# Decay bias rows made on GpSimd by one multiply-add instead of on ScalarE and VectorE

## The chip, the cores and the metric

The kernel runs on one core of a Trainium2 chip. The metric is the device time of one launch in microseconds (us); smaller is better. Engine names are those of the profile: PE is TensorE's matmul side and PEld its weight load, DVE is VectorE, ACT is ScalarE, POOL is GpSimd, SP is SyncE, which here only issues DMAs.

## What is computed

Attention with a decay bias (batch 8, 8 heads, 576 tokens, head width 64), followed by a gated feed forward (512 to 1536 to 512) over the 4608 tokens:

```python
scores = matmul(q, k.T) / sqrt(D)
cum    = cumsum(maximum(s, 0), axis=-1)
bias   = -(cum[..., :, None] - cum[..., None, :])       # query i, key j: cum[j] - cum[i]
scores = where(j > i, -1e9, scores + minimum(bias, 0))
attn   = softmax(scores) ; x = attn @ v                 # heads side by side: 4608 x 512
out    = ((sigmoid(x @ w_gate) * (x @ w_val)) @ w_out)
```

`cum` never falls along the tokens, so at every key that a query may see (j <= i) the bias is at most 0 before the minimum is taken, up to rounding.

## The kernel before, in words

There are 64 heads (8 batches of 8). A head is worked in five query tiles of 64, 128, 128, 128 and 128 queries, which see 64, 192, 320, 448 and 576 keys. One tile is one tick of the loop at L643, so there are 320 ticks, and three stages of a tile lie one tick apart: the score products on PE (`s_part`, L358) with the bias row (`bias_part`, L369); the sum of scores and bias with its extreme on DVE (L385) and the exponential on ACT (L390), both in `max_part`; the split of the weights into fp16 high and low parts (L401 to L404) and their transposes by DMA in `p_part`. The value products (`av_part`, L415) come a head later.

The first batch, heads 0 to 7, goes another way in float32, with functions whose names begin with `n_` (`n_bias` L494, `n_max` L502), because the feed-forward weights are prepared in the same stretch of time: per hidden block, loads, squares on ACT (L224), a sum over the partitions on POOL (`partition_all_reduce`, L228), and the split on DVE and ACT (L231 to L245). The sum over the partitions is also used for each pair of later heads, to find the scale of q and k (`qk_square`, L297), and once per batch for v (L143). That is 12, 28 and 8 of them.

From batch 1 on, the feed forward of the batch before is worked beside the attention: 216 units in all (18 groups of 256 tokens by 12 hidden blocks), each of 24 matmuls at L586, a tanh on ACT (L591), a product on DVE (L593), a split on ACT and DVE (L596, L597) and 6 matmuls at L610 three units later. The schedule gives some three units to a head. The last batch's feed forward stands alone at the end. Results leave by DMAs issued on POOL (L615), which also issues the loads of v for its squares (L138).

**The bias row.** For head i and query tile t, a row of `cum` (`crow`, loaded onto all partitions by L338) is combined with one value per partition, the query's own `cum`. Heads 8 to 63 (`bias_part`): ACT computes `relu(cf * crow + bc)` (L374), with `cf` and `bc` from `qk_scale`, in the units of the scaled scores and with the sign turned. Heads 0 to 7 (`n_bias`): DVE computes `min(crow - cumT, 0)` (L497). In both, POOL then fills the part of the last 64 or 128 columns above the diagonal with a large value (`affine_select`, L375 and L498), and DVE reads the row at L385 or L508. The rows have the tag `rl`, two buffers, which the loads of v at L138 share.

**What sets the order.** The Python code gives the emission order and marks some pieces as urgent (`first()`); a scheduler then places each engine's instructions. Every engine works its own list strictly in that order. Around the bias row the lists to watch are POOL's (row, diagonal fill, sums over the partitions, DMA issues), DVE's (L385 stands among the feed forward's L593 and L597) and PE's (score products among feed-forward units). Scores have three PSUM banks, the products `gv` of L586 two.

Of the kernel before, what the change touches and what calls it, by code (L numbers as in the profile page):

```python
# [17 lines left out]
P = 128  # L18
GT = 256          # tokens of one feed-forward group
PSCALE = 2.0 ** 14  # scale of the split softmax weights  # L20
# [4 lines left out]
def tile_attention_then_gated_ffn(  # L25
# [19 lines left out]
    QP = 96                  # tokens per chunk of q and k  # L45
    QC = S // QP
    # query tiles: (first query, queries, keys seen)
    TILES = [(0, 64, 64)] + [(64 + 128 * i, 128, 192 + 128 * i) for i in range(4)]
    NTL = len(TILES)
    QA = 320                 # queries of the first half of the value product  # L50
    QB = S - QA
    JA, JB = 3, 5            # key blocks of the two halves
    HI_ACT = (2, 3, 4)       # query tiles whose high weights ScalarE writes
    NN = H                   # heads computed in float32
    LAG = 3                  # units between the two products of the feed forward
# [15 lines left out]
    w1 = [cp.tile([P, NC, 2, 2, P], F16, name=f"w1_{f}") for f in range(NF)]   # chunk, gate/val, hi/lo  # L71
    w2 = [cp.tile([P, 2, DM], F32R, name=f"w2_{f}") for f in range(NF)]        # hi/lo
# [10 lines left out]
    expo = cp.tile([P, 2], F32, name="expo")     # exponents of -scale(q) and scale(k)  # L83
# [7 lines left out]
    nc.gpsimd.memset(cumT, 0.0)  # L91
    cum_d = dp.tile([NH, S], F32, name="cum_d")
# [4 lines left out]
    def field(ss, n, tag):  # L97
        """Exponent field of the power of two that brings a norm (from its square) to 2**15 at most."""
        e = wp.tile([P, n], I32, tag=f"xe{n}", name=f"xe_{tag}")
        f_ = wp.tile([P, n], I32, tag=f"xf{n}", name=f"xf_{tag}")  # L100
        nc.vector.tensor_scalar(e, ss.bitcast(I32), 23, None, ALU.logical_shift_right)
        nc.vector.tensor_scalar(f_, e, -0.5, 204.75, ALU.mult, ALU.add)
        return f_
# [19 lines left out]
    for t, (q0, m, w) in enumerate(TILES):  # L123
        ps = score_bank(f"pct{t}")
        nc.tensor.transpose(ps[:m, :NH], cum[:, q0 : q0 + m], ident[:NH, :NH])
        nc.vector.tensor_copy(cumT[:m, t, :], ps[:m, :NH])

# [1 line left out]
    vch = H * S * D // P // S      # chunks of a batch of v  # L129
    vview = v.rearrange("b h s d -> b (h s d)").rearrange("b (c p n) -> b c p n", c=vch, p=P)  # L130
    sv = {}        # batch -> (scale, inverse)
# [33 lines left out]
    scb = {}       # batch -> [P, 2, NF] factors of the gate and value products  # L165
# [3 lines left out]
    # staging: two buffers of their own, and the last weights' room until they come  # L169
# [34 lines left out]
    def decode_weight(n):  # L204
        """float32 from the words of a float64: exponents below the normal range end at zero."""
# [94 lines left out]
    def qk_scale(p):  # L300
# [8 lines left out]
        cf = wp.tile([P, 3], F32, tag="qkcf", name=f"qkcf{p}")       # -1/c, 1/c, c  # L309
# [59 lines left out]
    def bias_part(i, t):  # L369
        q0, m, w = TILES[t]  # L370
        p, j = divmod(i, 2)
        sc, cf, bc = qkc[p]
        r = wp.tile([P, S], F32, tag="rl", name=f"rl{i}_{t}")
        nc.scalar.activation(r[:m, :w], crow[i][:m, :w], AF.Relu, bias=bc[:m, t, j : j + 1], scale=cf[:m, 0:1])  # L374
        nc.gpsimd.affine_select(r[:m, q0:w], r[:m, q0:w], pattern=[[-1, m]], compare_op=ALU.is_ge,  # L375
                                fill=MASKED, base=0, channel_multiplier=1)
        rl[i, t] = r
# [81 lines left out]
    def n_prep(p):  # L459
        """Transposes of q (a tile per head, the other head's rows zero) and k of a pair of heads."""  # L460
# [33 lines left out]
    def n_bias(i, t):  # L494
        q0, m, w = TILES[t]
        r = wp.tile([P, S], F32, tag="rl", name=f"rl{i}_{t}")
        nc.vector.tensor_scalar(r[:m, :w], crow[i][:m, :w], cumT[:m, t, i : i + 1], 0.0, ALU.subtract, ALU.min)  # L497
        nc.gpsimd.affine_select(r[:m, q0:w], r[:m, q0:w], pattern=[[-1, m]], compare_op=ALU.is_ge,  # L498
                                fill=-MASKED, base=0, channel_multiplier=1)
        nB[i, t] = r  # L500
# [138 lines left out]
    NE, NOFF = 44, 80        # ticks: the feed forward begins, and has caught up  # L639
    FPT = 1.5                # units of the feed forward in a tick when it begins  # L640
    WLA = 3                  # hidden blocks whose weights are made ahead
    nticks = NTL * NH
    for n in range(nticks + 6):  # L643
# [17 lines left out]
        # value products of the head before  # L661
# [5 lines left out]
        # preparation of the heads to come  # L667
# [48 lines left out]
        # feed forward of the batch before  # L716
# [16 lines left out]
        b = m // (NTL * H) if m >= 0 else 0    # batches whose heads have all been written  # L733
# [39 lines left out]
```

## Time and profile before

| what | us |
|---|---|
| three runs | 1253.43, 1255.73, 1258.74; median 1255.73 |
| span of the profiled execution, first to last instruction | 1250.6 |
| busy in it: PE, PEld | 1168.5, 928.8 |
| busy in it: ACT, DVE | 979.2, 910.2 |
| busy in it: POOL | 180.0 |

The profiled execution has no timed run of its own; its span is 5.1 us under the median of the runs. "Busy" is the time in which an engine's instructions ran; a matmul's end is modelled. Groups are named by line, engine, operation and tiles (out<-in). In a timeline row the first number is the start in us from the beginning of the span, the second the time that the row's instructions took, and the bracket the engine's idle time ahead of it with what ended it ("issue": nothing that the profile shows). In a row of windows each engine's busy us come with the count of its instructions, then the granted clock of TensorE as a share, the share of the DMA engines that is busy, and GB/s.

### The profile page before, as it was taken

How to read it: one execution, taken by the hardware profiler on the slowest of the kernel's cores; microseconds unless marked ns; L12 is line 12 of the kernel's file. 1: busy time of each engine (PE TensorE's matmuls, PEld its weight loads, DVE VectorE, ACT ScalarE, POOL GpSimd, SP SyncE). 2: the span in 40 equal slices, each digit the busy share in tenths (PEclk: the TensorE clock that was granted, in tenths of full speed). 3: DMA queues.
4: the chain of work that ended last, by engine and by line, in shares of the span. 5: the costliest groups of instructions: out<-in, count | busy, mean ns of one | idle time of the engine just before them, and what ended most of it. 6: DMA issues, size and time to landing. Idle time of an engine off the chain costs nothing. (4 is left out here: it accounts for less than half of the span.)

```text
span 1250.6 us, 26501 instructions
## 1 busy us (share of the span) xinstructions
PE 1168.5 (93%) x8581; PEld 928.8 (74%) x8581; DVE 910.2 (73%) x3167; ACT 979.2 (78%) x2453; POOL 180.0 (14%) x463
## 2 busy tenths in 40 slices
PE   2688979999999999999999999999999999999997
PEld 1566757776777777788888877777778788888885
DVE  5898889788889787877676677878888788522221
ACT  4888879899989898988777688889998998533221
POOL 2333111111111121110111011111121111000000
PEclk9788789999999999999999999999999999999999
DMA  8765788778897898865475488768887865200000
GB/s 230 216 182 156 171 159 167 156 135 160 165 172 137 141 169 152 163 135 123 118 128 120 84 156 150 155 133 163 155 165 140 150 136 120 44 18 17 2 18 17
DMA packets 434731, 164.98 MB, mean 132 GB/s; under 512 B 400928, under 2 KB 420384, under 8 KB 434592
## 3 DMA queue, kind: packets, MB, share of 16 engines
q1 hardware_dynamic: 414752, 125.53, 54.2%
q0 software_dynamic: 5440, 18.88, 5.1%
q10 hardware_dynamic: 14400, 18.88, 5.1%
q8 instruction: 67, 1.10, 0.4%
q14 instruction: 72, 0.59, 0.2%
HBM read 75.64 MB, written 9.58 MB: 68 GB/s over the span
## 5 line engine op out<-in xcount | busy, mean ns | idle before, releaser
L586 PE MATMUL gv<-xg,w 128*128 128x256 f16 x5184 | 618.9, 274 | 3.1 <-ACT xg L562 1.6
L586 PEld LDWEIGHTS <-w 128*128 128x128 f16 x5184 | 496.8, 98 | 85.9 <-issue 20.9
L610 PE MATMUL o<-w,h 128*128 128x512 f32 x1296 | 360.0, 411 | 2.6 <-ACT osb L614 2.6
L610 PEld LDWEIGHTS o<-w,h 128*128 128x128 f32 x1296 | 227.2, 189 | 43.0 <-ACT osb L614 3.5
L591 ACT ACTIVATE th<-gv,scb 128x256 f32<-128x256 f32 (+3 forms) x288 | 111.2, 412 | 98.2 <-PE gv L586 96.8
L375 POOL TENSOR_SCALAR_AFFINE_SELECT rl<-rl 64x64 f32<-64x64 f32 x280 | 91.7, 328 | 668.9 <-ACT rl L374 524.6
L404 DVE SCALAR_TENSOR_TENSOR p<-e,er,p 64x128 f16<-64x128 f32 (+1 forms) x280 | 169.9, 613 | 17.2 <-ACT p L401 14.6
L374 ACT ACTIVATE rl<-cr,qkb,qkcf 64x64 f32<-64x64 f32 x280 | 180.0, 643 | 0.6 <-DVE em L385 0.4
L390 ACT ACTIVATE e<-e,em 64x64 f32<-64x64 f32 x280 | 154.8, 553 | 17.6 <-DVE em L385 16.8
L593 DVE SCALAR_TENSOR_TENSOR t<-th,gv 128x256 f32<-128x256 f32 x216 | 89.2, 413 | 102.3 <-ACT th L591 101.5
L596 ACT ACTIVATE h<-t,scb 128x256 fp32r<-128x256 f32 (+3 forms) x288 | 121.5, 447 | 41.6 <-DVE t L593 41.4
L597 DVE SCALAR_TENSOR_TENSOR h<-t,scb,h 128x256 fp32r<-128x256 f32 (+3 forms) x288 | 114.8, 412 | 50.1 <-ACT h L596 48.1
L385 DVE CUSTOM_DVE_ANT_0 e<-s,rl,qkcf 64x64 f32<-64x64 f32 x280 | 132.8, 482 | 20.9 <-PE s L366 12.9
L401 ACT ACTIVATE p<-e,er 128x384 f16<-128x384 f32 x168 | 118.8, 711 | 1.3 <-ACT e L390 0.9
L424 PEld LDWEIGHTS <-v 128*128 128x128 f16 (+1 forms) x896 | 79.4, 97 | 44.3 <-issue 16.5
L365 PE MATMUL s<-T 128*64 128x64 f16 x336 | 92.9, 289 | 7.4 <-DVE em L385 5.0
L366 PE MATMUL s<-T 128*64 128x64 f16 x336 | 92.5, 281 | 6.3 <-DMA T<-T 6.3
L294 ACT ACTIVATE jq<-qk 96x768 f16<-96x768 f32 x56 | 46.9, 837 | 35.2 <-DMA qk<-in_q_dram 33.9
L424 PE MATMUL av<-ptb,v 128*128 128x256 f16 (+2 forms) x560 | 64.2, 252 | 10.4 <-DVE x L431 5.7
L365 PEld LDWEIGHTS <-T 128*64 128x64 f16 x336 | 33.2, 99 | 53.1 <-issue 44.4
L396 DVE TENSOR_SCALAR er<-es 64x1 f32<-64x1 f32 x280 | 40.9, 147 | 32.3 <-ACT e L390 29.0
L431 DVE SCALAR_TENSOR_TENSOR x<-av,xh 64x320 f32<-64x320 f32 x112 | 50.7, 453 | 16.6 <-ACT xh L430 14.8
(152 smaller groups left out, 1253.3 us busy)
## 6 DMA issues: line engine op xcount, KB each, us to landing
cr<-cum_d SPq DMA_DIRECT2D x64, 288.0 KB, 3.8
vsq<-in_v_dram POOLq DMA_DIRECT2D x32, 288.0 KB, 3.8
out_dram<-osb POOLq DMA_DIRECT2D x36, 256.0 KB, 3.4
v<-in_v_dram SPq DMA_DIRECT2D x64, 128.0 KB, 2.7
qk<-in_q_dram SPq DMA_DIRECT2D x28, 288.0 KB, 3.9
qk<-in_k_dram SPq DMA_DIRECT2D x28, 288.0 KB, 4.8
T<-T SPq DMA_DIRECT2D x112, 72.0 KB, 2.1
ws<-in_moe_w_out_dram ACTq DMA_DIRECT2D x8, 512.0 KB, 4.5
```

What stands on the lines that cost most here:

```text
L365: nc.tensor.matmul(ps[:m, : b_ - a], lhs, T[i][:, 1, a:b_], start=True, stop=False)
L374: nc.scalar.activation(r[:m, :w], crow[i][:m, :w], AF.Relu, bias=bc[:m, t, j : j + 1], scale=cf[:m, 0:1])
L385: nc.vector.tensor_tensor_reduce(e_t[t][:m, a:b_], ps[:m, : b_ - a], rl[i, t][:m, a:b_], c, init, ALU.add, ALU.min, acc[:m])
L390: nc.scalar.activation(e_t[t][:m, :w], e_t[t][:m, :w], AF.Exp, bias=init, scale=-1.0, accum_out=sm[:m])
L401: nc.scalar.activation(hi, e, AF.Copy, scale=d[:m, 1:2])
L404: nc.vector.scalar_tensor_tensor(p_t[t][:m, :, 1], e, d[:m, 1:2], hi, ALU.mult, ALU.subtract)
L424: nc.tensor.matmul(ps[:, lo:n], lhs, PT[i][half][:kk, kb, hl, lo:n], start=(kb == 0 and hl == 0), stop=(kb == nj - 1 and hl == 1))
L586: nc.tensor.matmul(ps[:, gv, :n], w1[f][:, cc, gv, wl], xg[g][:, cc, xl, :n], start=(c == 0), stop=(c == 3 * NC - 1))
L591: nc.scalar.activation(th[:, a:e], ps[:, 0, a:e], AF.Tanh, scale=scb[b][:, 0, f : f + 1])
L596: nc.scalar.activation(h[:, 0, a:e], t2[:, a:e], AF.Copy, scale=scb[b][:, 1, f : f + 1])
L597: nc.vector.scalar_tensor_tensor(h[:, 1, a:e], t2[:, a:e], scb[b][:, 1, f : f + 1], h[:, 0, a:e].bitcast(F32), ALU.mult, ALU.subtract)
L610: nc.tensor.matmul(ps[:m], h[:, hl, tt * P : tt * P + m], w2[f][:, wl], start=(f == 0 and c == 0), stop=(f == NF - 1 and c == 2))
```

## The change

Both ways to make the bias row become one `tensor_scalar` on POOL with two per-partition values. In `bias_part` it is `crow * cf + bc`, without the relu; in `n_bias` it is `crow * 1 + cumN`, without the minimum, where `cumN` is `-cumT` of the first eight heads, made once on DVE. The diagonal fill stays behind it on POOL. Nothing else in the code differs but comments.

```diff
     cumT = cp.tile([P, NTL, NH], F32, name="cumT")
     nc.gpsimd.memset(cumT, 0.0)
+    cumN = cp.tile([P, NTL, NN], F32, name="cumN")
...
         nc.vector.tensor_copy(cumT[:m, t, :], ps[:m, :NH])
+    nc.vector.tensor_scalar(cumN, cumT[:, :, :NN], -1.0, None, ALU.mult)
...
         r = wp.tile([P, S], F32, tag="rl", name=f"rl{i}_{t}")
-        nc.scalar.activation(r[:m, :w], crow[i][:m, :w], AF.Relu, bias=bc[:m, t, j : j + 1], scale=cf[:m, 0:1])
+        nc.gpsimd.tensor_scalar(r[:m, :w], crow[i][:m, :w], cf[:m, 0:1], bc[:m, t, j : j + 1], ALU.mult, ALU.add)
         nc.gpsimd.affine_select(r[:m, q0:w], r[:m, q0:w], pattern=[[-1, m]], compare_op=ALU.is_ge,
                                 fill=MASKED, base=0, channel_multiplier=1)
...
         r = wp.tile([P, S], F32, tag="rl", name=f"rl{i}_{t}")
-        nc.vector.tensor_scalar(r[:m, :w], crow[i][:m, :w], cumT[:m, t, i : i + 1], 0.0, ALU.subtract, ALU.min)
+        nc.gpsimd.tensor_scalar(r[:m, :w], crow[i][:m, :w], 1.0, cumN[:m, t, i : i + 1], ALU.mult, ALU.add)
         nc.gpsimd.affine_select(r[:m, q0:w], r[:m, q0:w], pattern=[[-1, m]], compare_op=ALU.is_ge,
                                 fill=-MASKED, base=0, channel_multiplier=1)
```

The code's lines behind `cumN` stand two or three numbers later in the changed kernel: L228 becomes L230, L297 becomes L299, L375 becomes L378, L385 becomes L388.

POOL's list near the beginning, before: the first sum over the partitions (`wtot`) and the first bias rows of head 0 (`rl`). A row that says only "ISA" is an instruction without tiles.

```order
L228 ISA
L228 ISA wtot0_572<-wss0_476 128x2
L498 AFFINE_SELECT rl0_0_203<-rl0_0_203 64x64
L498 AFFINE_SELECT rl0_1_212<-rl0_1_212 128x128
L138 DMA vsq0_0_230<-in_v_dram 128x576
L498 AFFINE_SELECT rl0_2_235<-rl0_2_235 128x128
L138 DMA vsq0_1_246<-in_v_dram 128x576
L228 ISA wtot1_874<-wss1_779 128x2
```

The same place in the changed kernel:

```order
L230 ISA
L230 ISA wtot0_574<-wss0_478 128x2
L500 ISA
L500 TENSOR_SCALAR rl0_0_205<-cr0_170,cumN_125 64x64
L500 TENSOR_SCALAR rl0_1_214<-cr0_170,cumN_125 128x192
L501 AFFINE_SELECT rl0_0_205<-rl0_0_205 64x64
L501 AFFINE_SELECT rl0_1_214<-rl0_1_214 128x128
L140 DMA vsq0_0_232<-in_v_dram 128x576
L500 TENSOR_SCALAR rl0_2_237<-cr0_170,cumN_125 128x320
L501 AFFINE_SELECT rl0_2_237<-rl0_2_237 128x128
L230 ISA
L230 ISA wtot1_876<-wss1_781 128x2
```

Besides the multiply-adds, the change puts a bare ISA row ahead of the first multiply-add behind a sum over the partitions, and another ahead of each sum that follows a multiply-add. Before, there is one such row ahead of the first sum, one ahead of the very first `affine_select` (`ident`, a helper's line) and one at the program's start; `affine_select` and the sums then stand side by side without any.

POOL's list in the middle, before: the end of head 27 and the start of head 28, with the sum for heads 30 and 31 (`qkt15`).

```order
L375 AFFINE_SELECT rl27_3_6882<-rl27_3_6882 128x128
L297 ISA qkt15_7269<-ssq1_119 128x2
L375 AFFINE_SELECT rl27_4_6960<-rl27_4_6960 128x128
L375 AFFINE_SELECT rl28_0_7033<-rl28_0_7033 64x64
L375 AFFINE_SELECT rl28_1_7061<-rl28_1_7061 128x128
```

The same place in the changed kernel:

```order
L378 AFFINE_SELECT rl27_3_6884<-rl27_3_6884 128x128
L140 DMA vsq4_1_6912<-in_v_dram 128x576
L377 TENSOR_SCALAR rl27_4_6962<-cr27_6495,qkcf13_6229,qkb13_6233 128x576
L299 ISA
L299 ISA qkt15_7271<-ssq1_119 128x2
L378 AFFINE_SELECT rl27_4_6962<-rl27_4_6962 128x128
L377 ISA
L377 TENSOR_SCALAR rl28_0_7035<-cr28_6780,qkcf14_6790,qkb14_6794 64x64
L378 AFFINE_SELECT rl28_0_7035<-rl28_0_7035 64x64
L377 TENSOR_SCALAR rl28_1_7063<-cr28_6780,qkcf14_6790,qkb14_6794 128x192
```

Here a bare row stands ahead of the sum and another behind the diagonal fill of `rl27_4`, so two consecutive bias rows (`rl27_4`, `rl28_0`) each have one in front. In the whole list there are 47 bare rows at the lines of the sums (11, 28 and 8 of them at L230, L299 and L145) and 47 at those of the multiply-adds (11 at L500 and 36 at L377).

DVE's list at the same place in the changed kernel, from the product of a feed-forward unit on (`t2`, `h` are the feed forward's, `e_4` with `rl27_4` is the sum of scores and bias):

```order
L596 SCALAR_TENSOR_TENSOR t2_4_7_6943<-th4_7_6940,gv4_7_6915 128x256
L388 ISA e_4_94,em27_4_0_7040<-s27_4_0_6956,rl27_4_6962,qkcf13_6229 128x288
L388 ISA em27_4_0_7040 128x1
L407 SCALAR_TENSOR_TENSOR p16_3_98<-e_3_93,er27_3_7046,p16_3_98 128x4x128
L388 ISA e_4_94,em27_4_1_7042<-s27_4_288_6959,rl27_4_6962,em27_4_0_7040,qkcf13_6229 128x288
L388 ISA em27_4_1_7042 128x1
L600 SCALAR_TENSOR_TENSOR h4_7_6945<-t2_4_7_6943,scb1_3570,h4_7_6945 128x128
```

It is nearly the list of before: the sum that reads the bias row stands ahead of the feed forward's next split (`h4_7`). On PE, from head 19 on, the count of feed-forward matmuls ahead of a tile's score product is that of before or at most 24 matmuls, one unit, off.

## The prediction

> **What bounds the kernel now.** I read the page's first part, then the windows of three stages: the first batch with the weights (A), the attention of batches 1 to 7 beside the feed forward (B), and the last feed forward alone (C).
>
> ```profile
> span 1250.6 us, 26501 instructions
> PE 1168.5 (93%) x8581; PEld 928.8 (74%) x8581; DVE 910.2 (73%) x3167; ACT 979.2 (78%) x2453; POOL 180.0 (14%) x463
> 30.00:140.00 110.00, 88.32 (x465) 68.06 (x466) 98.43 (x332) 93.71 (x256) 33.44 (x62) 0.83 0.64 175
> 140.00:1085.00 945.00, 916.26 (x6936) 728.00 (x6937) 758.50 (x2709) 826.94 (x2062) 136.86 (x367) 0.99 0.75 145
> 1085.00:1251.00 166.00, 157.47 (x1160) 128.98 (x1158) 37.64 (x93) 46.73 (x112) 4.35 (x8) 0.98 0.04 14
> ```
>
> In A, DVE is busy for 98.43 of 110 us, and TensorE's granted clock is 0.83. In B, PE is busy for 916.26 of 945 us at clock 0.99, while ACT (88%) and DVE (80%) keep up. So B, three quarters of the span, is set by PE, and an engine matters there only where PE comes to wait for it. POOL works for 14% of the time; but it works its list in order, and every bias row goes through it.
>
> **What leaves ACT and DVE.** The groups, of DVE and of ACT:
>
> ```profile
> L497 DVE TENSOR_SCALAR rl<-cr,cumT 64x64 f32<-64x64 f32 (+4 forms) x40 | 14.7, 377 | 4.4 <-ACT vsq L139 4.4
> L374 ACT ACTIVATE rl<-cr,qkb,qkcf 64x64 f32<-64x64 f32 x280 | 180.0, 643 | 0.6 <-DVE em L385 0.4
> ```
>
> DVE loses 40 instructions, 14.7 us, all in A; one small product for `cumN` comes back, under half a us by the 377 ns of this row. ACT loses 280 instructions, 180.0 us, all in B. What that could bring at most: in A the 14.7 us, since DVE is the bound there; in B not the 180 but PE's idle 945 - 916.26 = 28.7 us. Together 43, and I would expect some 27 of them (the 14.7, and under half of PE's gaps, as many of those wait for transfers or other products).
>
> **What POOL gets: the multiply-adds.** The trace has none on POOL. Its nearest rows there are the diagonal fill, which also reads and writes a float32 row, and the fills of constants:
>
> ```profile
> L375 POOL TENSOR_SCALAR_AFFINE_SELECT rl<-rl 128x128 f32<-128x128 f32 x224 | 76.0, 340 | 568.3 <-ACT rl L374 458.0 <-DVE er L397 32.1 <-DVE p L404 17.1
> L375 POOL TENSOR_SCALAR_AFFINE_SELECT rl<-rl 64x64 f32<-64x64 f32 x56 | 15.7, 280 | 100.6 <-ACT rl L374 66.7 <-DVE er L397 31.9 <-DVE er L396 1.4
> L468 POOL MEMSET nq<- 64x576 f32 x8 | 4.8, 611 | 1.4 <-PE s L491 1.2
> L91 POOL MEMSET cumT<- 128x320 f32 x1 | 0.4, 354 | 0.0
> ```
>
> From 64 to 128 columns the fill grows by 60 ns, 0.94 ns a column on a start of 220; the constants grow by (611 - 354) / 256 = 1.0 ns. At 0.94 the five multiply-adds of a head (64 to 576 columns, 1600 in all) take 5 x 220 + 1600 x 0.94 = 2.6 us. That is an estimate, its lower end the start alone (1.1 us), its upper end twice it (5.2). Even the upper end with the fills of a head ((76.0 + 15.7) / 56 = 1.6 us) is 6.8 us of the 945 / 56 = 16.9 us that a head takes in B. By themselves the multiply-adds fit, and cost nothing on the path: POOL makes a row while PE works for the tile before.
>
> **What POOL gets beside them: the bare rows.** This carries the forecast. A sum over the partitions and a multiply-add never follow each other without a bare ISA row between. Before, there is one ahead of `ident` and one ahead of the first sum. POOL's timeline shows what follows them:
>
> ```profile
> 1.77 0.10 POOL L85 MEMSET expo<- 128x1 f32 x1
> 13.71 0.28 POOL masks.py:199 TENSOR_SCALAR_AFFINE_SELECT ident<-ident 128x128 f32<-128x128 f32 x1 [11.84 <-issue]
> 14.44 2.51 POOL L468 MEMSET nq<- 64x576 f32 x4
> 23.62 0.50 POOL L228 PARTITION_ALL_REDUCE wtot<-wss  x1 [6.67 <-ACT nk L481]
> ```
>
> Between the end of the constants and `ident`, whose row in the order stands right behind the first bare row, POOL stands still for 11.84 us, with nothing that the profile would show as waited for. Behind the second, it stands still for 6.67 us, to 16.95 + 6.67 = 23.62. There the squares that the sum needs came late as well:
>
> ```profile
> 23.09 0.19 ACT L224 ACTIVATION_READ_ACCUMULATOR w<-w 128x1 f32 x1
> ```
>
> They end at 23.28, so 6.67 us is an upper bound for that row and no price. I read a bare row as a change of POOL's set of operations. The Trainium skill states it so (GPSIMD Engine Reference, section Instruction dispatch): operation libraries are loaded at run time, and the first call to a freshly loaded one pays some 6 us (5.95 measured) with no instruction of its own in the profile. The gap of 11.84 us marked "issue" agrees in kind and is twice as long; no row here separates a load in the middle of the kernel.
>
> The transfers were busier behind the first bare row than in B, which I take as the reason to expect less than 11.84 later:
>
> ```profile
> 2.00:12.00 10.00, 0.00 (x0) 0.00 (x0) 2.34 (x3) 2.61 (x3) 0.00 (x0) 1.00 1.07 314
> 17.00:23.30 6.30, 2.87 (x10) 1.69 (x10) 4.92 (x10) 5.04 (x13) 0.00 (x0) 1.00 0.78 221
> ```
>
> The DMA share was 1.07 there, 0.78 behind the second and is 0.75 in B. Prices: the row ahead of a sum, between 0 and 6.67 us, taken as 6; the row ahead of a multiply-add, between 0 and 11.84, taken as 8, between the two gaps and nearer to the one at B's DMA share. A pair is 14 us, bounds 0 to 18.5. By the Trainium skill's 5.95 (the section just named) for each it would be 11.9 us.
>
> **How much of a pair is covered.** A bias row is ready shortly before DVE takes it. For two rows of head 27 (POOL's fill, then DVE's sum):
>
> ```profile
> 448.90 0.29 POOL L375 TENSOR_SCALAR_AFFINE_SELECT rl<-rl 128x128 f32<-128x128 f32 x1 [0.55 <-ACT rl L374]
> 450.63 0.42 DVE L385 CUSTOM_DVE_ANT_0 e<-s,rl,qkcf 128x192 f32<-128x192 f32 x1
> 454.35 0.30 POOL L375 TENSOR_SCALAR_AFFINE_SELECT rl<-rl 128x128 f32<-128x128 f32 x1 [5.16 <-ACT rl L374]
> 454.94 0.55 DVE L385 CUSTOM_DVE_ANT_0 e<-s,rl,qkcf 128x320 f32<-128x320 f32 x1
> ```
>
> The lead is 1.4 and 0.3 us. That this was no hindrance shows in the waits of DVE (us in total, times, longest):
>
> ```profile
> DVE e L385 <- POOL rl L375: 5.3, 8, 2.9
> ```
>
> Two `rl` buffers allow at most two tiles, 2 x 945 / 280 = 6.8 us. When DVE waits at L385, the feed forward's L593 and L597 stand behind it on DVE, so PE runs out of free `gv` banks after about one more unit, whose 24 matmuls take 2.8 us:
>
> ```profile
> 450.32 2.78 PE L586 MATMUL gv<-xg,w 128*128 128x256 f16 x24
> ```
>
> So between 0.3 and 6.8 + 2.8 = 9.6 us of a pair is hidden; I take 5. Where a pair lies in front of two consecutive bias rows, as for `rl27_4` and `rl28_0`, its parts add up, as DVE has one tile to work in between. After it PE cannot make up anything: it was the bound.
>
> **The sum.** B has 36 pairs (the bare rows at L377), each worth 14 - 5 = 9 us: 324. A has 11 (L500): 99. A's gain on DVE and ACT's relief count nothing here, since both then wait. PE's clock: at A's share of idle time it was 0.83, in B 0.99. With 324 us of waits B falls toward A's state; 0.94 would cost 916.26 x (0.99 / 0.94 - 1) = 49, nothing and 916.26 x (0.99 / 0.83 - 1) = 177 being the ends; I take 50. The span is 1250.6 + 324 + 99 + 50 = 1723.6, and with the 5.1 us between the span and the median of the runs 1729, forecast as 1730. By the Trainium skill's 11.9 us a pair (the same section) the same sum is 1250.6 + 47 x 6.9 + 50 + 5.1 = 1630.
>
> **The rivals.**
>
> *The bare rows are cheap, and the change wins.* For it: the 11.84 us stand at the start, where the transfers are at their busiest and where much happens once; the 6.67 us hide behind ACT. Then the row costs less than the cover, POOL has room, A loses 14.7 us of DVE, and B some of PE's gaps: 1255.73 - 27 = 1229. It decides where a pair takes less than about 5 us in the middle of the kernel. Against it: nothing else stands in that gap of 11.84 us. Chance 0.06.
>
> *The bare rows are cheap, but POOL and DVE get in each other's way.* Diagonal fills took longer in A than in B:
>
> ```profile
> L498 POOL TENSOR_SCALAR_AFFINE_SELECT rl<-rl 128x128 f32<-128x128 f32 x32 | 18.1, 576 | 34.3 <-DVE rl L497 26.0 <-DVE xg__326 L110 2.6 <-DVE xf_w L102 1.7
> L404 DVE SCALAR_TENSOR_TENSOR p<-e,er,p 64x128 f16<-64x128 f32 (+1 forms) x280 | 169.9, 613 | 17.2 <-ACT p L401 14.6
> ```
>
> The same fill took 576 ns instead of 340, beside a DVE that hardly rested. If each of the 320 multiply-adds holds an instruction of DVE like L404 up for such a 0.24 us, or is held up by it, that is 76 us: 67 of them in B, where DVE would be at 758.5 + 67 = 826 of 945 and PE still the bound, and 9 in A, which take most of the 14.7 back. The result is 1250, no difference to be measured. The Trainium skill has the rule (SBUF — State Buffer, section Who interferes with whom): a DVE instruction with two SBUF inputs and a GpSimd instruction that reads SBUF take turns over a shared port, the later one waiting fully. It bears on this rival alone. Chance 0.05, of which 0.02 with a visible loss.
>
> *POOL becomes the bound.* If both kinds of bare row cost what the trace shows at the start, a pair takes 18.5 us: 47 x 13.5 = 635, and with the clock at 0.90 another 916.26 x (0.99 / 0.90 - 1) = 92, so 1250.6 + 635 + 92 + 5.1 = 1983. In A alone the 11 pairs would be 204 us of POOL, in a stage of 110. Chance 0.17.
>
> **How the numbers follow.** The forecast has 0.72. Its own range goes from 9.5 us a pair (47 x 4.5 = 212 and 25 for the clock: 1490) to 16.5 (47 x 11.5 = 541 and 90: 1890). The range that should hold the time 8 times in 10 goes on to the third rival's value, 1990, and below to 1440, a pair of 9 us with no loss of clock; the two cheap rivals and the outer parts of the others are left out, some 0.2. About 0.5% is what a measurement of this kernel can tell from no change. Faster by more: 0.06, the first rival. Within it: 0.03, of the second. Slower: 0.72 + 0.17 + 0.02 = 0.91.
>
> **What would show it.** On POOL, idle time of several us ahead of each first multiply-add behind a sum, and ahead of each sum, marked "issue" or put down to an instruction long done; the multiply-adds themselves at 0.3 to 0.8 us. On DVE, a long wait of L388 for POOL's `rl`, against 5.3 us before. In B, PE busy for some 73% instead of 97%, gaps of 5 to 12 us near the end of every second head, and a granted clock under 0.99. ACT's busy time falls by 180 us with no gain. The forecast is wrong if POOL goes on within 2 or 3 us of a bare row, if the gaps lie elsewhere than behind them, or if multiply-adds take several us each.

## The result, and the profile after

The changed kernel takes 1620.74 us (median, 1615.26 to 1621.96) where the kernel before takes 1254.58 (1249.35 to 1258.74). The ratio is 1.2898, 95% interval 1.2853 to 1.2943: it is slower by 29%, some 366 us. The profiled execution spans 1619.3 us, 368.7 more than that of before.

The page of the changed kernel, its first part, and then the windows of the three stages, with edges at the same events as before (first batch, batches 1 to 7, last feed forward). The columns are those of the windows above: PE, PEld, DVE, ACT, POOL, granted clock, DMA share, GB/s.

```profile
span 1619.3 us, 26532 instructions
PE 1252.9 (77%) x8581; PEld 978.4 (60%) x8581; DVE 917.2 (57%) x3128; ACT 853.0 (53%) x2173; POOL 445.6 (28%) x783
```

```profile
30.00:255.00 225.00, 114.00 (x472) 88.00 (x471) 95.64 (x304) 100.10 (x267) 56.46 (x101) 0.59 0.31 90
255.00:1453.00 1198.00, 973.00 (x6924) 756.44 (x6923) 766.95 (x2694) 693.32 (x1770) 378.04 (x645) 0.91 0.59 113
1453.00:1619.00 166.00, 158.19 (x1166) 129.47 (x1163) 37.95 (x93) 46.83 (x113) 4.35 (x8) 0.99 0.04 14
```

No engine is busy for more than 77% of the time. Stage A has grown by 115 us (225 against 110), B by 253 (1198 against 945), C not at all. In B, PE is idle for 1198 - 973 = 225 us against 28.7 before, 196 more, and its same work takes 973 - 916 = 57 us longer, at clock 0.91 instead of 0.99. That is where the 368 us are.

What PE and DVE stand for is in the list of waits of the changed kernel, of which these are some lines (us in total, times, longest):

```profile
POOL rl L377 <- issue: 183.8, 26, 7.5
POOL qkt L299 <- issue: 148.0, 24, 7.2
DVE qk L304 <- POOL qkt L299: 122.2, 28, 6.6
PE s L367 <- DVE em L388: 97.3, 33, 9.0
DVE vso L147 <- POOL vst L145: 84.5, 8, 13.0
POOL wtot L230 <- issue: 64.4, 10, 7.6
POOL rl L500 <- issue: 64.2, 9, 8.1
DVE xe_w L102 <- POOL wtot L230: 56.6, 11, 6.7
DVE e L388 <- POOL rl L378: 51.2, 22, 7.2
DVE e L388 <- POOL rl L377: 20.0, 4, 7.0
```

In the kernel before, the first of the waits for a sum was short:

```profile
DVE qk L302 <- POOL qkt L297: 18.6, 19, 2.2
```

POOL stands still some 6 to 8 us at a time for "issue", at the lines of the multiply-adds (L377, L500) and of the sums (L299, L230, L145). In the trace's records, from the bare row to the next instruction, it is 5.8 us (median) ahead of a sum and 7.1 ahead of a multiply-add, 47 of each: 12.9 us a pair. DVE stands mostly for the sums: L304, L147 and L102 add up to 263 us, against 25 before, while its wait for the bias row itself (L388) is 51.2 and 20.0, 71 us. PE then waits for DVE's `em`.

No row shows what POOL does in these gaps: the two DMA queues of instructions move 67 and 72 packets in the kernel before and in the changed one alike, though the changed one has 92 more such gaps. "Load" below is the prediction's reading of them; what the trace shows is the bare row and the time until the next instruction.

One pair in the middle, on POOL's timeline (start, us, what it was, idle before it and what ended that):

```profile
1207.72 0.82 POOL L377 TENSOR_SCALAR rl<-cr,qkcf,qkb 128x576 f32<-128x576 f32 x1
1214.99 0.41 POOL L299 PARTITION_ALL_REDUCE qkt<-ssq  x1 [6.45 <-issue]
1215.29 0.36 POOL L378 TENSOR_SCALAR_AFFINE_SELECT rl<-rl 128x128 f32<-128x128 f32 x1
1223.23 0.56 POOL L377 TENSOR_SCALAR rl<-cr,qkcf,qkb 64x64 f32<-64x64 f32 x1 [7.59 <-ACT qk L327]
```

The first gap, 6.45 us, stands at the change to the sums' set, the second, 7.59 us, at the change back. The second is put down to an instruction of ACT, L327, which scales q and k and writes nothing that this multiply-add reads: so a load can hide in a list of waits behind another engine's name. DVE in the same time:

```profile
1209.36 0.14 DVE L400 RECIPROCAL er<-er 128x1 f32<-128x1 f32 x1
1215.43 0.24 DVE L304 TENSOR_SCALAR qk<-qkt 128x2 int32<-128x2 int32 x1 [5.92 <-POOL qkt L299]
...
1225.49 0.42 DVE L388 CUSTOM_DVE_ANT_0 e<-s,rl,qkcf 128x192 f32<-128x192 f32 x1 [0.58 <-POOL rl L378]
```

And PE:

```profile
1211.11 1.14 PE L427 MATMUL av<-ptb,v 128*128 128x256 f16 x10
1212.19 2.80 PE L589 MATMUL gv<-xg,w 128*128 128x256 f16 x24
1214.74 1.64 PE L613 MATMUL o<-w,h 128*128 128x512 f32 x6
...
1217.62 0.24 PE L367 MATMUL s<-T 128*128 128x192 f16 x1 [1.06 <-DVE em L388]
...
1224.96 0.35 PE L367 MATMUL s<-T 128*128 128x448 f16 x1 [2.71 <-DVE em L388]
```

While DVE stands for the sum, PE still has value products, one feed-forward unit and the second products of another, and it runs dry at the end of that and again at the end of the second load: here 1.06 + 2.71 = 3.8 us of the two gaps reach it.

The groups of POOL's two operations at the later heads (count, then busy us, mean ns, idle before; a group is named by its smallest shape):

```profile
L377 POOL TENSOR_SCALAR rl<-cr,qkcf,qkb 64x64 f32<-64x64 f32 x280 | 228.0, 817 | 535.0 <-DVE em L388 258.3
L378 POOL TENSOR_SCALAR_AFFINE_SELECT rl<-rl 64x64 f32<-64x64 f32 x280 | 107.7, 393 | 10.8
```

A multiply-add takes 817 ns in the mean, 4.1 us a head, and the fill behind it 393 ns where it took 328.

### The profile page after: what moved, and what is told of

Same layout as the page of the kernel before. It is cut to its first block, busy times and chain, and to the rows that moved or that the text cites. A ratio compares the mean times of both kernels' runs of the same rounds, so it can differ in the third digit from the quotient of the medians.

```text
span 1619.3 us, 26532 instructions
## 1 busy us (share of the span) xinstructions
PE 1252.9 (77%) x8581; PEld 978.4 (60%) x8581; DVE 917.2 (57%) x3128; ACT 853.0 (53%) x2173; POOL 445.6 (28%) x783
## 5 line engine op out<-in xcount | busy, mean ns | idle before, releaser
L589 PE MATMUL gv<-xg,w 128*128 128x256 f16 x5184 | 646.3, 282 | 25.3 <-DVE t L596 12.8
L589 PEld LDWEIGHTS <-w 128*128 128x128 f16 x5184 | 510.1, 101 | 119.4 <-issue 31.2
L613 PE MATMUL o<-w,h 128*128 128x512 f32 x1296 | 367.3, 419 | 54.5 <-ACT osb L617 54.5
L377 POOL TENSOR_SCALAR rl<-cr,qkcf,qkb 64x64 f32<-64x64 f32 x280 | 228.0, 817 | 535.0 <-DVE em L388 258.3
L613 PEld LDWEIGHTS o<-w,h 128*128 128x128 f32 x1296 | 233.9, 194 | 108.2 <-ACT osb L617 66.0
L388 DVE CUSTOM_DVE_ANT_0 e<-s,rl,qkcf 64x64 f32<-64x64 f32 x280 | 132.0, 481 | 86.9 <-POOL rl L378 51.2
L367 PE MATMUL s<-T 128*64 128x64 f16 x336 | 97.3, 301 | 100.5 <-DVE em L388 97.3
L427 PEld LDWEIGHTS <-v 128*128 128x128 f16 (+1 forms) x896 | 86.4, 104 | 85.4 <-issue 55.5
L494 PE MATMUL s<-nk,nq 128*128 128x288 f32 (+4 forms) x96 | 50.5, 641 | 84.6 <-DVE em L511 82.3
L378 POOL TENSOR_SCALAR_AFFINE_SELECT rl<-rl 64x64 f32<-64x64 f32 x280 | 107.7, 393 | 10.8
L427 PE MATMUL av<-ptb,v 128*128 128x256 f16 (+2 forms) x560 | 70.5, 267 | 44.5 <-DVE x L434 29.8
L368 PE MATMUL s<-T 128*64 128x64 f16 x336 | 96.5, 295 | 2.7 <-DMA T<-T 2.7
L494 PEld LDWEIGHTS s<-nk,nq 128*128 128x128 f32 (+1 forms) x96 | 22.0, 279 | 97.4 <-DVE em L511 90.2
```

The costliest lines, as they stand in the source:

```text
L368: nc.tensor.matmul(ps[:m, : b_ - a], lhs, T[i][:, 2, a:b_], start=False, stop=True)
L377: nc.gpsimd.tensor_scalar(r[:m, :w], crow[i][:m, :w], cf[:m, 0:1], bc[:m, t, j : j + 1], ALU.mult, ALU.add)
L388: nc.vector.tensor_tensor_reduce(e_t[t][:m, a:b_], ps[:m, : b_ - a], rl[i, t][:m, a:b_], c, init, ALU.add, ALU.min, acc[:m])
L427: nc.tensor.matmul(ps[:, lo:n], lhs, PT[i][half][:kk, kb, hl, lo:n], start=(kb == 0 and hl == 0), stop=(kb == nj - 1 and hl == 1))
L589: nc.tensor.matmul(ps[:, gv, :n], w1[f][:, cc, gv, wl], xg[g][:, cc, xl, :n], start=(c == 0), stop=(c == 3 * NC - 1))
L613: nc.tensor.matmul(ps[:m], h[:, hl, tt * P : tt * P + m], w2[f][:, wl], start=(f == 0 and c == 0), stop=(f == NF - 1 and c == 2))
```

## The experiments

Theory 1 is the prediction's: the price is the loading of POOL's sets of operations, wherever a sum and a multiply-add follow each other. Theory 2, the rival: the price is the multiply-adds themselves, because POOL and DVE hold each other up (the second rival of the prediction, at several times its price), or because POOL makes the rows later than ACT did. All ratios are against the kernel before on the same chip.

**The sums moved to PE, so that nothing is switched.** Two kernels: the changed one, and the one before as its control, each with every sum over the partitions made by two matmuls with ones and a copy on DVE. For q and k this sum also moves, from `qk_square` to `qk_scale`.

```diff
+    def total(tot, src, n, name):
+        ps = pp.tile([P, 512], F32, tag="gv", name=f"sum_{name}")
+        for h_ in range(2):
+            nc.tensor.matmul(ps[64 * h_ : 64 * h_ + 64, :n], ones, src, start=True, stop=True)
+        nc.vector.tensor_copy(tot, ps[:, :n])
...
-        nc.gpsimd.partition_all_reduce(tot, vss[b], P, ADD_REDUCE)
+        total(tot, vss[b], vch, f"v{b}")
```

> The changed kernel with all 48 sums over the partitions taken off POOL: each is a float32 product with a matrix of ones on TensorE and a copy on DVE, so that POOL keeps the multiply-adds and has no bare row between kinds of operations. Theory 1 (the time went into the changes of POOL's set of operations, 5.8 and 7.1 us each by the trace): nothing is left to wait for, the loss of 366 us goes altogether, and the kernel stands at 1225 to 1255 us, a little under before if the relief of ScalarE and VectorE is worth anything. Theory 2 (the multiply-adds themselves are too slow on POOL, 0.82 us a piece, or hold VectorE's two-input instructions up at the memory port): the loss stays for the most part, 1450 us or more. In between, 1300, would say that both take a share.

> Control: the kernel before with the same sums on TensorE and nothing else changed, so bias rows as before on ScalarE and VectorE. Both theories: within 1% of before, 1243 to 1262 us. What e1 differs from this one by is the multiply-adds' own effect, without any change of operation sets.

Measured: 1388.07 us for the changed kernel (ratio 1.1059, 1.1002 to 1.1116) and 1363.2 for the control (1.0874, 1.0827 to 1.0922). The control misses its range by 100 us, so the edit does something of its own, and the first number can't be read by itself. What it does is in the control's windows:

```profile
270.00:300.00 30.00, 30.00 (x229) 24.72 (x227) 6.83 (x15) 7.35 (x15) 0.99 (x2) 1.00 0.05 19
300.00:400.00 100.00, 59.26 (x322) 35.70 (x321) 67.57 (x265) 74.31 (x180) 12.13 (x36) 0.64 0.75 139
```

From 270 to 300 us PE does the feed forward alone while DVE and ACT have next to nothing; then PE is idle for 40 of the next 100 us at clock 0.64. The scheduler had drawn the feed forward of several hundred matmuls ahead of attention (576 of them ahead of head 12's first score product, 204 in the kernel before). The pair shows only that the two kernels lie 25 us apart where no set is switched.

**The switches alone.** The kernel before, its bias rows untouched, with one multiply-add of a single column on POOL behind each sum. The lists then have 76 bare rows at the sums and these multiply-adds, against 94 in the changed kernel.

```diff
+    def small_op(tot):
+        nc.gpsimd.tensor_scalar(tiny[:, 2:3], tot[:, 0:1], tiny[:, 1:2], tiny[:, 1:2], ALU.mult, ALU.add)
...
         nc.gpsimd.partition_all_reduce(tot, vss[b], P, ADD_REDUCE)
+        small_op(tot)
```

> The kernel before, bias rows on ScalarE and VectorE, with one multiply-add of a single column on POOL behind each sum over the partitions (its result is used nowhere). The order then has 75 bare rows beyond those at the program's ends, against 94 in the changed kernel, and POOL's extra work itself is some 48 x 0.2 = 10 us. Theory 1: the loss comes without any bias row moved, in proportion to the rows: 75 / 94 x 366 = 292, so 1545 us, 1450 to 1600 allowed. Theory 2: no difference from before, 1245 to 1265 us.

Measured: 1548.12 us, ratio 1.2344 (1.2277 to 1.2410), which is 294 us more than before. The waits:

```profile
POOL tiny L84 <- issue: 239.5, 33, 8.1
DVE qk L311 <- POOL qkt L305: 143.9, 26, 12.8
POOL qkt L305 <- issue: 90.0, 14, 7.5
DVE e L394 <- POOL rl L384: 99.6, 27, 7.6
```

48 instructions of one column make the kernel 23% slower, with the same kind of gaps. Theory 1 holds, and theory 2 can't make this time at all.

294 of 366 us is 0.80, and 76 of 94 bare rows is 0.81, but that the two agree so well is chance. Stages A and B of this kernel:

```profile
30.00:157.00 127.00, 87.38 (x446) 69.59 (x446) 77.42 (x265) 79.44 (x223) 26.49 (x59) 0.72 0.48 128
157.00:1382.00 1225.00, 978.83 (x6939) 752.72 (x6938) 773.90 (x2762) 844.95 (x2084) 168.85 (x413) 0.89 0.58 113
```

By the trace's records, B has 70 bare rows in both kernels, and it grows by 280 us here and by 253 in the changed one. A has 5 here and grows by 17 us; it has 22 in the changed kernel and grows by 115. What a load costs thus depends on where it stands. In B the switches alone cost no less than the whole change; why they cost more was not tested.

**One part of the change at a time.** The multiply-adds for heads 0 to 7 alone, and for heads 8 to 63 alone.

```diff
 heads 0 to 7 alone, in bias_part:
-        nc.gpsimd.tensor_scalar(r[:m, :w], crow[i][:m, :w], cf[:m, 0:1], bc[:m, t, j : j + 1], ALU.mult, ALU.add)
+        nc.scalar.activation(r[:m, :w], crow[i][:m, :w], AF.Relu, bias=bc[:m, t, j : j + 1], scale=cf[:m, 0:1])
 heads 8 to 63 alone, in n_bias:
-        nc.gpsimd.tensor_scalar(r[:m, :w], crow[i][:m, :w], 1.0, cumN[:m, t, i : i + 1], ALU.mult, ALU.add)
+        nc.vector.tensor_scalar(r[:m, :w], crow[i][:m, :w], cumT[:m, t, i : i + 1], 0.0, ALU.subtract, ALU.min)
```

> The change for heads 0 to 7 alone (bias rows by multiply-add there, on ScalarE for heads 8 to 63): 22 bare rows between kinds of operations, 11 pairs, all in the first batch. Theory 1: the loss of the first stage in the changed kernel's trace, 226 us between the sums of head 0 and head 8 against 110, so 1254 + 116 = 1370 us, 1340 to 1390. Theory 2 (multiply-adds too slow): 40 of the 320 multiply-adds, 366 / 8 = 46 us, 1300.

> The change for heads 8 to 63 alone (VectorE makes the rows of heads 0 to 7): 72 bare rows, 36 pairs, nearly all after the first batch. Theory 1: the rest of the loss, 366 - 116 = 250, so 1504 us, 1480 to 1530; the two parts add up, as the pairs do not overlap. Theory 2: 7/8 of 366, 1575 us.

Measured: 1371.33 us (1.0925, 1.0881 to 1.0968) and 1517.84 us (1.2079, 1.2033 to 1.2124): 116 and 261 us more than before, 377 together, against 366 for the whole. Windows of the two, stages A and B of each:

```profile
30.00:257.00 227.00, 111.06 (x468) 84.70 (x469) 96.46 (x306) 100.10 (x267) 57.84 (x106) 0.62 0.32 92
257.00:1209.00 952.00, 917.15 (x6933) 726.59 (x6933) 753.09 (x2697) 821.40 (x2052) 140.01 (x365) 0.99 0.77 142
```

```profile
30.00:136.00 106.00, 83.24 (x457) 64.72 (x455) 92.92 (x313) 90.78 (x247) 33.46 (x57) 0.82 0.66 172
136.00:1350.00 1214.00, 970.20 (x6929) 753.84 (x6929) 775.17 (x2710) 697.04 (x1780) 376.73 (x648) 0.90 0.58 112
```

Each part costs its own stage about what the changed kernel loses there (117 and 269 us, against 115 and 253), and the other stage 7 us or less. 40 of the 320 multiply-adds, an eighth, bring 116 of 377 us, nearly a third: the loss doesn't go by their number.

**The scale taken up a tile later.** In the changed kernel DVE stands behind the sum at L304. This one emits `qk_scale`, and `split_qk` behind it, one tick later.

```diff
-                if t == 0:
+                if t == 1:
                     qk_scale(p + 1)
-                if t == 1:
+                if t == 2:
                     split_qk(i + 1)
```

> The changed kernel with the scale of a pair's q and k (and the split behind it) one tick later in the emission, so that VectorE asks later for the sum that POOL delivers late. In the changed kernel VectorE waited 122 us for these sums (28 times), a wait that the prediction did not name. Theory 1a (the wait for the sum is where the first half of a pair costs): up to 28 x 3 = 84 us come back, 1535 to 1590 us. Theory 1b (the bias rows behind the load come late anyway, and VectorE then waits for those): no gain beyond 10 us, 1610 to 1625 us.

Measured: 1620.41 us (1.2925, 1.2853 to 1.2998). The wait is as it was, too, and the reason is plain from the order of DVE's instructions: L304 of every pair stands at the same place as in the changed kernel. The edit tested nothing but that the time repeats. Whether a later L304 would hide more of the first load is left open.

```profile
DVE qk L304 <- POOL qkt L299: 122.4, 28, 6.5
```

**The multiply-adds alone.** The changed kernel and, as its control, the one before, both without the 48 sums over the partitions: each partition's own part stands for the total, and this leaves out that part of the computation. No set is switched then.

```diff
-        tot = wp.tile([P, 2], F32, tag="qkt", name=f"qkt{p}")
-        nc.gpsimd.partition_all_reduce(tot, ss, P, ADD_REDUCE)
-        qkc[p] = tot
+        qkc[p] = ss
...
```

> The changed kernel with the 48 sums over the partitions left out (each partition's own part stands for the total, so scales differ by partition and the output isn't the reference's); multiply-adds on POOL as in the change, no bare row between kinds of operations. Unlike e1, TensorE gets nothing new and the feed forward's place among the heads stays that of the changed kernel. Theory 1 (changes of POOL's set of operations): the loss goes, 1225 to 1265 us. Theory 2 (the multiply-adds, 0.82 us each on POOL, or their hold on VectorE): most of the loss stays, 1450 us or more. Theory 3 (both): the multiply-adds alone cost some 20 to 100 us, 1280 to 1350.

> Control: the kernel before with the 48 sums left out in the same way, bias rows on ScalarE and VectorE. All theories: 1235 to 1255 us, at most some 10 us under before, since POOL then starts without the gap of 11.84 us at the first bare row. What f1 differs from this by is what the multiply-adds on POOL bring or cost by themselves.

Measured: 1277.1 us (1.0178, 1.0143 to 1.0213) and 1244.24 us (0.9912, 0.9881 to 0.9944). This control holds. The multiply-adds by themselves thus cost 33 us, and the loads the rest: 366 less 33 is 333 us, 91% of the loss. 25 of the 33 lie in stage B and 2 in A; the profiled executions are 28.5 us apart. The windows of stage B, first of the changed kernel and then of the one before, both without sums:

```profile
136.00:1107.00 971.00, 916.64 (x6926) 727.88 (x6925) 776.60 (x2696) 686.48 (x1770) 357.33 (x608) 0.99 0.73 139
```

```profile
134.00:1080.00 946.00, 916.72 (x6939) 726.97 (x6938) 759.24 (x2710) 823.63 (x2057) 119.76 (x330) 0.99 0.76 144
```

PE works the same 917 us at the same clock. DVE does the same work in 17 us more, and that ACT is busy for 137 us less brings nothing. PE waits 25 us more, 20 of it at the value products. The groups of DVE whose time changed, and PE's wait for the value product's buffer from the list of waits, in the same order of kernels:

```profile
L595 DVE SCALAR_TENSOR_TENSOR h<-t,scb,h 128x256 fp32r<-128x256 f32 (+3 forms) x288 | 122.1, 436 | 58.7 <-ACT h L594 56.3
L401 DVE TENSOR_SCALAR p<-e,er 64x128 f16<-64x128 f32 x112 | 44.1, 408 | 0.7 <-DVE er L394 0.3
...
PE av L422 <- DVE x L429: 22.3, 17, 2.6
```

```profile
L592 DVE SCALAR_TENSOR_TENSOR h<-t,scb,h 128x256 fp32r<-128x256 f32 (+3 forms) x288 | 114.8, 412 | 49.9 <-ACT h L591 48.0
L398 DVE TENSOR_SCALAR p<-e,er 64x128 f16<-64x128 f32 x112 | 33.8, 313 | 1.6 <-DVE er L391 0.3
...
PE av L419 <- DVE x L426: 2.0, 3, 1.3
```

**Where the 33 us come from.** Two more kernels without sums: the changed one with every multiply-add issued twice, and the one before with a multiply-add added behind each bias row, of the row's size, that writes `crow` back onto itself. For heads 8 to 63 DVE reads nothing of that; for heads 0 to 7 its next row does, and waits 0.2 us for it in all. The added multiply-add has two constants where the changed kernel's has two per-partition values, and is shorter (530 ns in the mean against 809). It stands ahead of the diagonal fill, so the row is finished later by its time.

```diff
 the changed kernel without sums, in bias_part and n_bias alike:
         nc.gpsimd.tensor_scalar(r[:m, :w], crow[i][:m, :w], cf[:m, 0:1], bc[:m, t, j : j + 1], ALU.mult, ALU.add)
+        nc.gpsimd.tensor_scalar(r[:m, :w], crow[i][:m, :w], cf[:m, 0:1], bc[:m, t, j : j + 1], ALU.mult, ALU.add)
 the kernel before without sums, behind the row of ACT or DVE:
+        nc.gpsimd.tensor_scalar(crow[i][:m, :w], crow[i][:m, :w], 1.0, 0.0, ALU.mult, ALU.add)
```

> The changed kernel without the sums (1277.1 us), with each of the 320 multiply-adds issued twice, the second over the first; each partition's own part still stands for the sum over the partitions. It asks where the 33 us come from by which that kernel stands above the one before without the sums (1244.2). Theory 1, POOL and DVE hold each other up, in proportion to what POOL works beside DVE: another 20 to 40 us, 1297 to 1317. Theory 2, the row reaches DVE later than ACT's did: the row is later by another 0.3 to 1.0 us, against a lead of some 3 us, so 1277 to 1290, with DVE's wait for POOL's rl growing from 2.0 us. Theory 3, only the other order that the scheduler found: 1267 to 1287, without a trend.

> The kernel before without the sums over the partitions (1244.2 us; each partition's own part stands for the sum), with one multiply-add on POOL per bias row added, of that row's size, that writes the row of cum back onto itself unchanged; ACT and DVE make the bias rows as before. DVE never reads what POOL adds. Theory 1, POOL and DVE hold each other up: some 33 us more, 1265 to 1285, with DVE's instructions that read two tiles in SBUF longer (313 ns to about 400 for the reduction p<-e,er). Theory 2, the row reaches DVE later because POOL makes it: no change, 1240 to 1255. Theory 3, the scheduler's order: 1240 to 1265, and DVE's instructions no longer.

Measured: 1299.5 us (1.0355, 1.0315 to 1.0395), 22 us over the changed kernel without sums, and 1257.45 us (1.0029, 1.0005 to 1.0053), 13 (by the medians) to 15 (by the ratios) over the one before without sums. From the page, the busy times, then DVE's group of the low parts `p<-e,er,p`, for the doubled kernel and then for the one with the added multiply-adds; for the doubled one also DVE's wait for the bias row:

```profile
PE 1174.2 (90%) x8581; PEld 929.8 (72%) x8581; DVE 954.6 (73%) x3128; ACT 845.9 (65%) x2173; POOL 667.8 (51%) x1055
L403 DVE SCALAR_TENSOR_TENSOR p<-e,er,p 64x128 f16<-64x128 f32 (+1 forms) x280 | 184.4, 665 | 17.8 <-ACT p L400 14.6
...
DVE e L384 <- POOL rl L374: 18.6, 32, 1.7
```

```profile
PE 1171.3 (93%) x8581; PEld 926.0 (74%) x8581; DVE 931.9 (74%) x3167; ACT 982.9 (78%) x2453; POOL 327.3 (26%) x735
L400 DVE SCALAR_TENSOR_TENSOR p<-e,er,p 64x128 f16<-64x128 f32 (+1 forms) x280 | 179.6, 646 | 18.8 <-ACT p L397 16.2
```

With its work unchanged, DVE is busy for 25 us more by the doubling (929.3 before it) and 20 more by the added multiply-adds (911.4), and the time rises by 22 and by 13 to 15. So POOL's multiply-adds lengthen what DVE does beside them, whether DVE reads their rows or not. Without and with the added ones, `p<-e,er,p` takes 613 and 646 ns and `h<-t,scb,h` 412 and 420, both of which read two tiles; the groups that read a PSUM bank, with one tile at most beside it, keep their time (`e<-s,rl,qkcf` 482 and 481, `t<-th,gv` 414 and 413, `x<-av,xh` 452 and 453).

How much of the 33 us this explains is less clear. (The theories named here are those of the two expectations above.) The doubled kernel falls in the first theory's range, but the second theory's sign came as well: DVE's wait for the row rose from 2.0 us to the 18.6 of the line above. The kernel with added multiply-adds stays under the first theory's range, 2 us over the second's and inside the third's; only DVE's longer instructions speak against the third. The group named for it, `p<-e,er`, went from 313 to 324 ns and not to 400. And the added multiply-adds cost some 6 us in each of the stages A and B, while the changed kernel without sums loses 25 in B. So the sharing is shown, with 13 to 15 us as the price of such multiply-adds in all; how the 33 us divide between it, the later row and the other order of the lists was not separated.

**The start.** A gap of 11.84 us stands ahead of `ident` in the kernel before and not in the changed one, where the gap ahead of the first sum is 13.07 us instead of 6.67. This kernel is the one before with one multiply-add of one column near the end, where POOL is idle.

```diff
...
                 nc.gpsimd.dma_start(out[g * GT + tt * P : g * GT + tt * P + m, :], o[:m])
+                if g == NG - 3 and tt == 0:
+                    nc.gpsimd.tensor_scalar(tiny[:m], o[:m, 0:1], 1.0, 0.0, ALU.mult, ALU.add)
```

> The kernel before with one multiply-add of one column on POOL, on a result tile of the third group from the end, where POOL is idle. It leaves the multiply-add's set of operations behind for the next launch. Theory 1, a set that is still there from the launch before isn't loaded again: the gap of 11.84 us ahead of ident at the start goes, the load moves to the first sum, which waits for squares until 23.3 us anyway, and the time falls by 4 to 11 us, to 1244 to 1251. Theory 2, the set is loaded at each launch's first use and the changed kernel's start had another reason: no change, 1251 to 1259, with the gap of some 12 us still ahead of ident.

Measured: 1251.72 us, ratio 0.9970 (0.9943 to 0.9997), and POOL's timeline at the start:

```profile
2.15 0.29 POOL masks.py:199 TENSOR_SCALAR_AFFINE_SELECT ident<-ident 128x128 f32<-128x128 f32 x1 [0.29 <-issue]
...
18.29 0.60 POOL L229 PARTITION_ALL_REDUCE wtot<-wss  x1 [13.17 <-DMA ws<-in_moe_w_val_dram]
```

The gap ahead of `ident` is gone, 0.29 us in place of 11.84, and the load stands ahead of the first sum. The 13.17 us there are no price of a load: in this kernel as in the changed one, the squares that the sum needs end 0.24 us before it starts. In the changed kernel that is, with the sum at 18.19:

```profile
17.76 0.19 ACT L226 ACTIVATION_READ_ACCUMULATOR w<-w 128x1 f32 x1
```

So a set that the launch before has left behind isn't loaded again. The other runs agree: the kernel with multiply-adds for heads 0 to 7 alone ends, like the one before, with the sums' set, and has the gap (11.55 us); the ones with multiply-adds for heads 8 to 63 and with the switches alone end with the multiply-adds' set and have 0.29 us there.

The mechanism is the first theory's. Its time isn't decided: 1251.72 us is 3.4 (by the medians) or 3.8 us (by the ratio) under before, a little less than the 4 to 11 that the theory gave and still in the range of the second, and under what a measurement can well tell.

| kernel | ratio to before | us against before, by the ratio |
|---|---|---|
| changed (+366 by the medians) | 1.2898 | +364 |
| switches alone (76 of 94 bare rows) | 1.2344 | +294 |
| changed, heads 0 to 7 alone | 1.0925 | +116 |
| changed, heads 8 to 63 alone | 1.2079 | +261 |
| changed without sums | 1.0178 | +22 |
| the same, multiply-adds twice | 1.0355 | +45 |
| before without sums | 0.9912 | -11 |
| the same, multiply-adds added | 1.0029 | +4 |

## Why the prediction was right, and where it was off

**The carrying step held.** The bare rows cost several us each in the middle of the kernel, and 47 pairs of them set the time; only that POOL spends it loading is seen in no row. The kernel with nothing but switches shows it, and so do the two without sums: without a switch, 333 of the 366 us are gone. The first rival, cheap bare rows, is out: POOL goes on after 5.8 and 7.1 us, not after 2 or 3.

**Their price was nearly right.** 6 us was taken ahead of a sum and is 5.8; 8 ahead of a multiply-add and is 7.1; the pair is 12.9 instead of 14. The Trainium skill (GPSIMD Engine Reference, section Instruction dispatch) gives 5.95 us for the first call to a freshly loaded library: this case agrees for the sums and has 1.1 us more for the multiply-adds. The gap at the start was the wrong row to reach for. In the changed kernel no gap of that length can be put down to a load alone: its two longest, 13.1 us at the start and 12.6 at 446 us, end with something else that POOL's instruction needed, the squares of the first sum and a row buffer that DVE (L388) gave free. The next longest is 8.8 us.

**The mis-sized term is the cover.** The sum had 324 us of waits in B, 99 in A and 50 for the clock, 473 in all. Measured are 196, 115 and 57, 368 in all. In B a pair costs 196 / 36 = 5.4 us and not 9, so 7.5 us of it are hidden and not 5, inside the bounds of 0.3 to 9.6. Without the 25 us that the multiply-adds bring there by themselves, it is 171 / 36 = 4.8, and 8.1 hidden. Of the 128 us too many in B, 36 x 1.1 = 40 come from the price and the rest from the cover. PE's timeline above shows for one pair where more cover comes from: the prediction gave PE one unit's 24 matmuls (2.8 us) to work on while DVE stands, but its list also holds the second products of a unit (1.64) and value products (1.14). PE is busy for 973 of B's 1198 us, 81%, where 73% was expected. Its waits at the score products are 2.9 us in the mean of 33 and 9.0 at most, not 5 to 12.

That the prediction's other sum, with 11.9 us a pair, gave 1630 and so came within 10 us is luck: its price is 1.0 us too low and its cover too small, and the two errors cancel.

**The place of DVE's wait was wrong.** It was put at L388, which reads the bias row. It did grow there, from 5.3 us to 71 for POOL's rows, and in the first batch from 0.4 to 51 (L511: 31.2 for the fill and 20.0 for the multiply-add). But the waits for the late sum, at L304, L147 and L102, are 263. In the timeline above DVE comes to the sum's reader, L304, before it needs the next row, and so the first half of a pair meets it there. The prediction looked only at who waits for the row that was moved, and not at who waits for the instruction that it now delays.

**In A the third rival's mechanism is close to what happened.** POOL is busy for 56 us there, and the 22 gaps behind bare rows are some 148 more: 204 of 225 us. POOL is nearly the bound of that stage. PE's work takes 26 us longer there (114.0 us for the 88.3 of before, at clock 0.59 against 0.83), but PE is idle for half of the stage, so that this adds to the 115 us isn't shown.

**The multiply-adds aren't free.** A head's five take 4.1 us against the estimate of 2.6 and its upper end of 5.2. The shortest of each size add up to 3.0, so the estimate was near for the shortest; in the mean one takes 0.22 us more than the shortest of its size. "Cost nothing on the path" was wrong by 33 us, most of them in B. It is the second rival's mechanism beside the first theory's: DVE's instructions grow while POOL works, as the Trainium skill has it (SBUF — State Buffer, section Who interferes with whom), and the traces of the last kernels agree, with 20 us on DVE for 178 us of multiply-adds (148.3 and 29.8 us of POOL in the kernel that adds them). The rival's 0.24 us for each multiply-add is about what was lost, but it was lost mostly on POOL, where it costs little; DVE has 17 us more of it in B and not 67. How the 33 us divide is not settled.

**The reliefs brought nothing,** as predicted: even without a switch the changed kernel is 33 us slower than its control. The relief of ACT was also smaller than the 180 us of the rows that left it: ACT is busy for 853 us instead of 979, 126 less.

## What to carry to other kernels

Before an operation is moved to an engine, look in that engine's instruction list for what must be loaded between it and its new neighbours: here an instruction of 0.8 us brought 12.9 us of loading wherever it met a sum over the partitions, and POOL's busy share of 28% shows none of it. Then ask who waits for the neighbours that it delays, and not only who waits for what is moved. Here ACT, busy for 78% of the time, became 126 us less busy and the kernel gained nothing by it. To see what a switch costs, put the switch alone into the kernel before: 48 one-column instructions showed it, without the change itself.

## What the runs showed of the hardware

A set of POOL's operations stays loaded from one launch to the next: with the needed set left behind, the first bare row took 0.29 us in place of 11.84. A load ahead of a sum took 5.8 us and one ahead of a multiply-add 7.1 in the middle of the kernel. The one ahead of `ident` took 11.84 at the start, where the transfers were at their busiest (a share of 1.07 in the kernel before, against 0.59 in B of the changed one); that the transfers lengthen it is argued from this alone. `affine_select` brought no load behind either of the two. The shortest multiply-adds with two per-partition values took 0.38 us for 64 columns and 0.81 for 576, some 0.84 ns a column; with one such value and a constant they took 0.31 and 0.74, with two constants 0.23 and 0.66. In the mean of all sizes those of the later heads took 817 ns beside DVE.
